# Weight conversion through a PSUM bank, GpSimd's long steps in halves, and a new port model in the planner

## The chip, the cores and the metric

The kernel runs on one NeuronCore of a Trainium2 chip. The metric is the device time of one execution in microseconds (us), lower is better. The core has five engines that work side by side and meet at semaphores: TensorE (PE in the profile; PEld is its weight load), VectorE (DVE), ScalarE (ACT), GpSimd (POOL) and SyncE (SP, which issues the DMA transfers). SBUF is the working memory of 128 partitions. PSUM is the small memory that TensorE writes; this kernel uses it as 8 banks of 512 fp32 values per partition.

## The reference, cut to what matters

```python
def _attn_ref(q, k, v, omega):                 # q, k, v: (8, 8, 576, 64) fp32
    q_s, k_s = q * scale, k * scale
    def phi(x):                                # 128 random features
        h = np.einsum('bhsd,md->bhsm', x, omega) - np.sum(x * x, -1, keepdims=True) / 2.0
        return np.exp(h - np.max(h, -1, keepdims=True)) / np.sqrt(m)
    q_p, k_p = phi(q_s), phi(k_s)
    kv = np.einsum('bhsm,bhsd->bhmd', k_p, v)
    z = np.sum(k_p, axis=2)
    num = np.einsum('bhsm,bhmd->bhsd', q_p, kv)
    return num / (np.einsum('bhsm,bhm->bhs', q_p, z)[..., None] + 1e-06)

def _moe_ref(x, w_in, w_out):                  # x: (4608, 512), w_in: (512, 2048), w_out: (2048, 512)
    h = x @ w_in
    g = h * erf(softplus(h))
    return g @ w_out
```

The attention's output, laid out as 4608 tokens of 512 values, is the x of the second part. The two weight matrices arrive as 64-bit floats, and the kernel turns them into 32-bit ones on the chip.

## The kernel before, in words

**Work.** Eight batches of 576 tokens. A batch has four pairs of heads in the attention and then two phases (`ph`) of the expert layer, each over half of the 2048 hidden values. A phase has four blocks "f" (`plain1` or `gemm1`: x times w_in for 256 hidden values) and four blocks "e" (`gemm2`: the hidden values of the phase before, times w_out). Tiles of matmul results are named `h`, `hS`, `hA` (first product), `o` (second), `ppk`, `ppq`, `kvp`, `pt`, `nd` (attention). Every matmul of the expert layer is done as three, with each operand split into a high part and the rest (`xh`/`xl`, `gh`/`gl`, and two halves of a weight tile `w`).

**Weights.** There are 32 weight units of 128 x 512 values. On its first use a unit is made (`make`, line 347): SP loads its 64-bit words into `st`; `w_bias` (POOL or ACT) scales the high words into `wt`; VectorE shifts `wt` in place (`w_shift`, TENSOR_SCALAR), then joins sign and tail in place (`w_sign`, `w_tail`, SCALAR_TENSOR_TENSOR, two operands each, `st` and `wt`). `parts` (line 339) then writes the high part into `w` (`w_high`, ACT or POOL) and the rest (`w_rest`, VectorE or POOL), and SP stores `w` to DRAM (`wd`) for later fetches. The first three batches (`PLAIN`) use the units as they are; in the third, `make_sums` builds sums of units (`R`, `S`, `cS`), with which the later batches need seven products in place of eight.

**Between the products.** `chain` (line 615) runs softplus and erf on ScalarE (`gs`), then for each group `gate` (`hs` = `gs` x `hs`), `high` (`gh`) and `rest` (`gl` = `hs` - `gh`). Gate and rest take 128 x 1152 values and may run on VectorE or POOL. `square` in the attention (`uk`, `uq`, 64 x 1152) runs on POOL or ACT. `split` makes `xh`, `xl` and the differences `xc`.

**Order.** `build` lists operations with, for each engine that may run them, an estimated cost and a slack: the engine takes the operation only if it is due later than that (-1e9: always). `Plan.order` (line 132) simulates five engines and writes down one order for each, which the chip then follows exactly. A tile takes a slot from its pool, so PSUM's 8 slots (`ps`) are shared under caps: 4 banks for attention (5 for the first batch), 3 and 2 for the two products. Due times come from `starts`: `FIRST` per pair of the first batch, `START0` for the first expert matmul. The model knows that some VectorE steps suffer beside GpSimd:

```python
                    if e == "V" and o.name in SHARED:
                        dur += min(dur, max(0.0, until["G"] - now) / 2)
```

Of the kernel before, what the change touches and what calls it, by code (L numbers as in the profile page):

```python
# [19 lines left out]
P = 128  # L20
# [43 lines left out]

SHARED = ("wshift", "wsign", "wtail", "wrest", "wwhole", "wsum", "xsum", "xhigh", "xrest", "gate",
          "high", "rest")


# [17 lines left out]
class Plan:  # L88
# [43 lines left out]
    def order(self, slots, caps):  # L132
# [56 lines left out]
        while True:  # L189
            progress = True  # L190
            while progress:
                progress = False
                for e in engines:
                    if not idle[e]:
                        continue
                    skipped, chosen = [], None
                    while ready[e]:
                        item = heapq.heappop(ready[e])
                        o = item[2]
                        if o.start is not None:  # L200
                            continue
                        ok = can(o)
                        if ok and e == "A":
                            if lock is not None and o.set is not None and o.macro != lock:
                                ok = False
                        if ok:
                            slack = next(s for x, _, s in o.opts if x == e)
                            if e == "S":
                                ok = o.due - now < slack
                            elif o.due - now < slack and slack > -1e8:  # L210
                                ok = False
                        if ok:
# [12 lines left out]
                    if e == "V" and o.name in SHARED:  # L225

                        dur += min(dur, max(0.0, until["G"] - now) / 2)
                    o.eng, o.start = e, now
                    for t in o.alloc:
                        t.slot = free[t.pool].pop(0)  # L230
                        held[t.stream] += 1
                        nxt[t.stream] += 1
                    idle[e] = False
                    if e == "A":
                        if o.set is not None and o.set != table:
                            dur += COST["table"]
# [55 lines left out]
WHOLE = 8  # L292
PLAIN = 3
PAIR = 8.6
FIRST = 13.0
LEAD = 30.0
STEP1 = 14 * 3 * COST["mm"]
STEP2 = 48 * COST["mm"]
START0 = 4 * FIRST + 10


def build(emit):
# [33 lines left out]
              reads=[(t, (x, k)) for x in "hl" for k in range(2)], writes=[(d, 0)],  # L336
              plan=clock[0] + 10.0, size=P * HW * 8)

    def parts(t, src, keys):

        ks = range(2)
        pl.op("whigh", [("A", 0.63, -1e9), ("G", 0.72, 5.0)], lambda e: E.w_high(e, t, src),
              reads=keys, writes=[(t, ("h", k)) for k in ks])
        pl.op("wrest", [("V", 0.7, -1e9), ("G", 1.35, 3.0)], lambda e: E.w_rest(e, t, src),
              reads=keys + [(t, ("h", k)) for k in ks], writes=[(t, ("l", k)) for k in ks])

    def make(u, t):

        nm = "_".join(str(c) for c in u)
        st = pl.tile("gl", f"st{nm}", [P, HW, 2], I32, "st")  # L350
        pl.op("wload", [("S", 0.1, AHEAD)], lambda e: E.w_load(st, u),
              writes=[(st, 0), (t, "room")], size=P * HW * 8)
        w = pl.tile("gh", f"wt{nm}", [P, HW], I32, "wt")
        pl.op("wbias", [("G", 0.95, -1e9), ("A", 0.65, -1e9)], lambda e: E.w_bias(e, st, w),
              reads=[(st, 0)], writes=[(w, 0)])
        pl.op("wshift", [("V", 0.7, -1e9)], lambda e: E.w_shift(w), reads=[(w, 0)], writes=[(w, 0)])
        pl.op("wsign", [("V", 0.92, -1e9)], lambda e: E.w_sign(st, w), reads=[(st, 0), (w, 0)],
              writes=[(w, 0)])
        pl.op("wtail", [("V", 0.92, -1e9)], lambda e: E.w_tail(st, w), reads=[(st, 0), (w, 0)],
              writes=[(w, 0)])  # L360
        parts(t, lambda: w.ap.bitcast(F32).rearrange("p (k c) -> p k c", k=2), [(w, 0)])
        store(u, t)

    def unit(u, block=None):
# [12 lines left out]
    def make_sums(ph, fp, t0, t1):  # L377

        r = pl.tile("gh", f"R{ph}_{fp}", [P, 2, 2, BW], F32, "wt")
        for i, t in enumerate((t0, t1)):  # L380
            pl.op("wwhole", [("V", 0.7, -1e9), ("G", 1.35, 3.0)],
                  lambda e, i=i, t=t: E.w_whole(e, r.ap[:, i], t),
                  reads=[(t, (x, k)) for x in "hl" for k in range(2)], writes=[(r, i)])
        s = pl.tile("gl", f"S{ph}_{fp}", [P, 4, BW], F32, "st")
# [36 lines left out]
    def load(n, qk):  # L421
# [13 lines left out]
        for i in range(parts):  # L435
            keys = range(3) if parts == 1 else [i]
            f = 1.0 / parts
            pl.op("sq" + qk, [("A", 1.17 * f + .1, -1e9)] if n == 0 else
                  [("G", 2.35, -1e9), ("A", 1.2, -1e9 if n < 4 else 4.0)],
                  lambda e, i=i: E.square(e, u, qk, i, parts),  # L440
                  reads=[(u, ("x", c)) for c in keys], writes=[(u, ("s", c)) for c in keys])

# [49 lines left out]
    def attend(n, t0):  # L492
        a = pairs[n]
        x = xs[n] = pl.tile("xs", f"xs{a['nm']}", [P, 2, T])
        for j in range(2):
            for t in range(2):
# [8 lines left out]
                pl.op("ndlog", [("A", 0.46, -1e9)], lambda e, j=j, nd=nd, rc=rc: E.log_den(rc, nd, j),  # L505
                      reads=[(nd, 0)], writes=[(rc, 0)], set="exp")
                pl.op("ndexp", [("A", 0.44, -1e9)], lambda e, j=j, rc=rc: E.exp_den(rc, j),
                      reads=[(rc, 0)], writes=[(rc, 0)], set="exp")
# [106 lines left out]
    def chain(b, ph, fps):  # L615
# [12 lines left out]
                  reads=[(x["gs"], 0) for x in gr], writes=[(g["gs"], 0)], set="erf", macro=m)  # L628
        for fp, g in zip(fps, gr):
            four = [(g["hs"], (i, t)) for i in range(2) for t in range(2)]  # L630
            pl.op("gate", [("V", 1.45, -1e9), ("G", 2.8, 10.0)], lambda e, g=g: E.gate(e, g["gs"], g["hs"]),
                  reads=four + [(g["gs"], 0)], writes=four)
            g["gh"] = pl.tile("gh", f"gh{b}_{ph}_{fp}", [P, 2, 2, T], F32R, cap=4 if b < PLAIN or (b, ph) == (PLAIN, 0) else None)
            pl.op("high", [("V", 0.8, -1e9), ("A", 1.2, 3.0)], lambda e, g=g: E.high(e, g["gh"], g["hs"]),
                  reads=four, writes=[(g["gh"], 0)])
# [69 lines left out]
def tile_attention_moe(ctx: ExitStack, tc: tile.TileContext, qT, kT, vP, omT, w1, w2, out):  # L705
# [55 lines left out]
    def difference(e, dst, a, b):  # L761
        (pool if e == "G" else dve).tensor_sub(dst, a, b)

    def rows(j):

        return (slice(0, D), slice(D, P)) if j == 0 else (slice(D, P), slice(0, D))

    class Emit:
# [52 lines left out]
        def square(self, e, u, qk, i, parts):  # L821
            c = slice(i * S2 // parts, (i + 1) * S2 // parts)
            src, dst = (slice(D, P), slice(0, D)) if qk == "k" else (slice(0, D), slice(D, P))
            if e == "G":
                pool.tensor_mul(u.ap[dst, c], u.ap[src, c], u.ap[src, c])
            else:
                act.activation(u.ap[dst, c], u.ap[src, c], AF.Square)

# [73 lines left out]
            copy(e, h.ap[:, i:i + n, :], src())  # L902

        def x_rest(self, e, l, src, h, i, n):
            difference(e, l.ap[:, i:i + n, :], src(), h.ap[:, i:i + n, :].bitcast(F32))

        def gemm1(self, hp, u, k, xh, xl, xi, c, more, end):
            wh, wl = (u.ap[:, k, i, c * P:(c + 1) * P] for i in range(2))
# [14 lines left out]
            act.activation(gs.ap, gs.ap, AF.Erf)  # L923

        def gate(self, e, gs, hs):
            (pool if e == "G" else dve).tensor_mul(hs.ap, gs.ap, hs.ap)

        def high(self, e, gh, g):
            copy(e, gh.ap, g.ap)

        def rest(self, e, gl, g, gh):
            difference(e, gl.ap, g.ap, gh.ap.bitcast(F32))

        def gemm2(self, op, w, fi, gh, gl, i, t, f):
            b, c = divmod(fi, 2)
# [71 lines left out]
```

## Time and profile before

| | us |
|---|---|
| median of 3 runs | 1127.03 (1125.81 to 1129.01) |
| the profiled execution | 1128.78 |
| its span, first to last instruction | 1126.8 |
| TensorE busy (modelled) | 1086.5 |
| VectorE busy | 758.5 |
| ScalarE busy | 718.8 |
| GpSimd busy | 471.4 |

TensorE's busy time counts an instruction as busy until its modelled end, and matmuls overlap; the number of matmuls that a stretch of time holds is the safer measure. A row of a group reads: line, engine, operation, output<-inputs, shape, count | busy us, mean ns | idle time of the engine before it. Nearly all rows carry line 722, the helper through which every instruction is issued, so rows are told apart by tile names. A row of a tile's view has the shortest, median and longest duration in ns. A row of the timeline has start and duration in us. All times are counted from the first instruction.

### The profile page before, as it was taken

Reading aid. Unit: us, or ns where it says so; the run is one execution under the profiler, and the core shown is the slowest. Engines: PE = TensorE matmul, PEld = TensorE weight load, DVE = VectorE, ACT = ScalarE, POOL = GpSimd, SP = SyncE. Lnnn points to the kernel's source line nnn. Section 1 sums busy time; section 2 is a strip of 40 time slices with the busy share of each in tenths; the row PEclk is TensorE's granted clock in tenths of the full one; section 3 lists DMA queues with packets and bytes.
Section 4 is the critical chain, followed back from the end, with each engine's and each line's share of the span. In section 5 each row is a group of like instructions: output and inputs, shape, how many; then the busy total and the mean of one; then the engine's idle time right before and its main releaser. Section 6 shows DMA issues by size and latency. Waiting matters only on the chain.

```text
span 1126.8 us, 21431 instructions
## 1 busy us (share of the span) xinstructions
PE 1086.5 (96%) x8272; PEld 1074.4 (95%) x8272; DVE 758.5 (67%) x1229; ACT 718.8 (64%) x1360; POOL 471.4 (42%) x276
## 2 busy tenths in 40 slices
PE   7999898999998999979999999999999999999998
PEld 6899798999998989979999999999999999999998
DVE  5969988876396585875668547684658657584641
ACT  8868776776666666754767766576667765544430
POOL 5637747533184274640325424352344413251320
PEclk9989999999998999989999999999999999999999
DMA  8545576574456565647765766657666665657761
GB/s 221 182 134 206 176 263 219 196 266 155 154 173 221 189 213 192 220 136 257 220 214 193 231 226 227 214 181 237 219 226 200 209 216 189 217 197 273 254 236 59
DMA packets 70116, 231.26 MB, mean 205 GB/s; under 512 B 8288, under 2 KB 8672, under 8 KB 70016
## 3 DMA queue, kind: packets, MB, share of 16 engines
q1 hardware_dynamic: 69952, 229.84, 62.0%
q8 instruction: 66, 1.08, 0.4%
q14 instruction: 34, 0.28, 0.1%
q0 software_dynamic: 64, 0.07, 0.0%
HBM read 195.26 MB, written 34.60 MB: 204 GB/s over the span
## 4 chain that ended last, share of the span: by engine, by line
PE 84%; DVE 10%; issue 2%; ACT 2%; POOL 1%; DMA 1%; SPq 0%; DVEq 0%; POOLq 0%; ACTq 0%
PE o L722 33%; PE hS L722 11%; PE h L722 10%; PE hA L722 8%; PE kvp L722 5%; PE ppq L722 5%; PE ppk L722 5%; PE nd L722 4%; DVE wt L722 3%; PE pt L722 2%; DVE gl L722 1%; DVE S L722 1%; DMA st<-w 1%; DVE w L722 1%; DVE hs L722 1%
## 5 line engine op out<-in xcount | busy, mean ns | idle before, releaser
L722 PE MATMUL o<-gh,w 128*128 128x288 f32 x2048 | 443.8, 298 | 3.8 <-DVE w L722 3.7
L722 PEld LDWEIGHTS o<-gh,w 128*128 128x128 f32 x2048 | 338.9, 188 | 4.5 <-DVE w L722 4.3
L722 PE MATMUL o<-gl,w 128*128 128x288 f32 x1024 | 302.2, 295 | 0.0
L722 PEld LDWEIGHTS o<-gl,w 128*128 128x128 f32 x1024 | 192.6, 188 | 0.2
L722 PE MATMUL h<-xh,w 128*128 128x288 f32 x768 | 181.7, 307 | 6.1 <-ACT hs L722 6.1
L722 POOL TENSOR_TENSOR hs<-gs,hs 128x1152 f32<-128x1152 f32 x36 | 102.0, 2838 | 167.9 <-ACT gs L722 155.4
L722 PE MATMUL hS<-xh,wS 128*128 128x288 f32 x640 | 165.7, 304 | 2.3 <-DVE u L722 2.3
L722 PEld LDWEIGHTS h<-xh,w 128*128 128x128 f32 x768 | 132.7, 192 | 7.0 <-ACT hs L722 6.8
L722 ACT ACTIVATE fk<-ppk,mxk 128x128 f32<-128x128 f32 x288 | 83.3, 373 | 85.6 <-DVE mxk L722 85.4
L722 POOL TENSOR_TENSOR gl<-hs,gh 128x1152 fp32r<-128x1152 f32 x35 | 109.2, 3131 | 33.8 <-ACT gh L722 24.4
L722 ACT ACT_TABLE_LOAD x92 | 118.0, 1283 | 7.0 <-DVE hs L722 4.7
L722 PE MATMUL hA<-xh,w 128*128 128x288 f32 x480 | 122.2, 299 | 0.0
L722 PEld LDWEIGHTS hS<-xh,wS 128*128 128x128 f32 x640 | 115.2, 190 | 2.6 <-DVE u L722 2.6
L722 PE MATMUL h<-xl,w 128*128 128x288 f32 x384 | 114.6, 298 | 0.4 <-POOL xl L722 0.4
L722 ACT ACTIVATE fq<-ppq,mxq 128x128 f32<-128x128 f32 x288 | 83.2, 370 | 30.4 <-DVE mxq L722 29.6
L722 PE MATMUL hS<-xl,wS 128*128 128x288 f32 x320 | 95.0, 297 | 0.0
L722 POOL TENSOR_TENSOR uq<-uq 64x1152 f32<-64x1152 f32 x21 | 46.3, 2203 | 113.7 <-DMA uq<-qT 67.6
L722 DVE TENSOR_REDUCE mxk<-ppk 128x3 f32<-128x384 f32 x96 | 51.9, 553 | 58.1 <-PE ppk L722 57.5
L722 ACT ACTIVATE gh<-hs 128x1152 fp32r<-128x1152 f32 x52 | 59.2, 1162 | 45.5 <-DVE hs L722 22.6
L722 PEld LDWEIGHTS hA<-xh,w 128*128 128x128 f32 x480 | 86.0, 189 | 0.0
L722 DVE TENSOR_TENSOR os<-o,os 128x288 f32<-128x288 f32 x64 | 29.1, 455 | 81.0 <-PE o L722 80.7
L722 PE MATMUL ppk<-wk,uk 128*128 128x128 f32 x576 | 79.6, 282 | 4.0 <-DVE wk L722 4.0
(94 smaller groups left out, 2195.0 us busy)
## 6 DMA issues: line engine op xcount, KB each, us to landing
w<-wdw SPq DMA_DIRECT2D x184, 512.0 KB, 4.3
wS<-wdcS SPq DMA_DIRECT2D x80, 512.0 KB, 4.0
st<-w SPq DMA_DIRECT2D x32, 512.0 KB, 4.8
wdw<-w SPq DMA_DIRECT2D x32, 512.0 KB, 3.6
v<-vP SPq DMA_DIRECT2D x32, 325.0 KB, 3.2
w<-wdw SPq DMA_DIRECT2D x40, 256.0 KB, 3.6
out<-os SPq DMA_DIRECT2D x32, 288.0 KB, 3.8
uk<-kT SPq DMA_DIRECT2D x31, 288.0 KB, 3.8
```

The costliest lines, as they stand in the source:

```text
L722: return tc.keep_in_program_order(method(*args, **kwargs))
```

## The change

The shift writes its result into a tile of PSUM (`pw`, at most one at a time, from the same 8 slots), sign and tail work there in place, and high part and rest read it from there. GpSimd no longer takes either of the last two steps for these units; for the sums' units (`make_sums`) it still may. On GpSimd, gate, rest, square and the x rests of more than one block are issued as two instructions of half the size. The planner's model takes a VectorE step of `SHARED` to wait until the running piece on GpSimd ends, and a GpSimd step until VectorE's last such step ends. The three steps that now touch PSUM leave `SHARED`. Costs, due times and slacks get other values, and a running mean of how late matmuls are (`late`) is added where an operation's slack is tested.

```diff
-SHARED = ("wshift", "wsign", "wtail", "wrest", "wwhole", "wsum", "xsum", "xhigh", "xrest", "gate",
+PIECES = dict(gate=2, rest=2, sqk=2, sqq=2, xrest=2)
+SHARED = ("wrest", "wwhole", "wsum", "xsum", "xhigh", "xrest", "gate",
           "high", "rest")
...
-                            elif o.due - now < slack and slack > -1e8:
+                            elif o.due - now + late < slack and slack > -1e8:
...
+                    if e == "T":
+                        late += 0.1 * (max(0.0, now - o.due) - late)
                     if e == "V" and o.name in SHARED:
-                        dur += min(dur, max(0.0, until["G"] - now) / 2)
+                        dur += max(0.0, until["G"] - now) % piece
+                        port = now + dur
+                    elif e == "G":
+                        dur += max(0.0, port - now)
+                        piece = dur / PIECES.get(o.name, 1) + 1e-6
...
-FIRST = 13.0
+FIRST = 11.5
-START0 = 4 * FIRST + 10
+START0 = 4 * FIRST + 5
+GATES = 10.0
+RESTS = 6.0
+EARLY = (2, 0)
+PW = 1
+WHV = 0.0
+GATES0 = 10.0
+RESTS0 = 15.0
+SQN = 4
+SQG = -1e9
+SQA = 4.0
+WHG = 5.0
+WBG = -1e9
...
-    def parts(t, src, keys):
+    def parts(t, src, keys, psum=False):
-        pl.op("whigh", [("A", 0.63, -1e9), ("G", 0.72, 5.0)], ...
+        pl.op("whigh", [("A", 0.58, -1e9), ("V", 0.62, WHV)] if psum else
+              [("A", 0.63, -1e9), ("G", 0.7, WHG)], ...
-        pl.op("wrest", [("V", 0.7, -1e9), ("G", 1.35, 3.0)], ...
+        pl.op("wlow" if psum else "wrest",
+              [("V", 0.68, -1e9)] if psum else [("V", 0.68, -1e9), ("G", 1.3, 3.0)], ...
...
+        p = pl.tile("ps", f"pw{nm}", [P, HW], I32, "pw", PW)
+        pl.op("wshift", [("V", 0.6, -1e9)], lambda e: E.w_shift(p, w), reads=[(w, 0)],
+              writes=[(p, 0)])
+        pl.op("wsign", [("V", 0.72, -1e9)], lambda e: E.w_sign(st, p), reads=[(st, 0), (p, 0)],
+              writes=[(p, 0)])
+        pl.op("wtail", [("V", 0.72, -1e9)], lambda e: E.w_tail(st, p), reads=[(st, 0), (p, 0)],
+              writes=[(p, 0)])
+        parts(t, lambda: p.ap.bitcast(F32).rearrange("p (k c) -> p k c", k=2), [(p, 0)], True)
...
-            pl.op("gate", [("V", 1.45, -1e9), ("G", 2.8, 10.0)], ...
+            pl.op("gate", [("V", 1.36, -1e9), ("G", 2.75, GATES if (b, ph) >= EARLY else GATES0)], ...
-            pl.op("rest", [("G", 2.8, 6.0), ("V", 1.45, -1e9)],
+            pl.op("rest", [("G", 2.75, RESTS if (b, ph) >= EARLY else RESTS0), ("V", 1.36, -1e9)],
...
+    def halves(e, n):
+        return (slice(0, n // 2), slice(n // 2, n)) if e == "G" else (slice(0, n),)
...
-        def w_shift(self, w):
-            dve.tensor_scalar(w.ap, w.ap, 3, None, op0=ALU.logical_shift_left)
+        def w_shift(self, p, w):
+            dve.tensor_scalar(p.ap, w.ap, 3, None, op0=ALU.logical_shift_left)
...
         def gate(self, e, gs, hs):
-            (pool if e == "G" else dve).tensor_mul(hs.ap, gs.ap, hs.ap)
+            for i in halves(e, 2):
+                (pool if e == "G" else dve).tensor_mul(hs.ap[:, i], gs.ap[:, i], hs.ap[:, i])
```

`square`, `x_rest` and `rest` are halved on GpSimd in the same way as `gate`. The slack of a rest on GpSimd in the first two batches goes from 6 to 15; `GATES`, `GATES0`, `RESTS`, `SQG`, `SQN`, `SQA`, `WHG` and `WBG` hold the values that stood in the code before.

More of the change, by code (lines that the diff above doesn't have):

```diff
@@ L156, in order @@
         now, table, lock, bw = 0.0, "exp", None, 0.0
+        port, piece, late = 0.0, 1.0, 0.0
         count = 0
@@ L337, in store @@
               plan=clock[0] + 10.0, size=P * HW * 8)
-    def parts(t, src, keys):
+    def parts(t, src, keys, psum=False):
         ks = range(2)
-        pl.op("whigh", [("A", 0.63, -1e9), ("G", 0.72, 5.0)], lambda e: E.w_high(e, t, src),
+        pl.op("whigh", [("A", 0.58, -1e9), ("V", 0.62, WHV)] if psum else
+              [("A", 0.63, -1e9), ("G", 0.7, WHG)], lambda e: E.w_high(e, t, src),
               reads=keys, writes=[(t, ("h", k)) for k in ks])
-        pl.op("wrest", [("V", 0.7, -1e9), ("G", 1.35, 3.0)], lambda e: E.w_rest(e, t, src),
+        pl.op("wlow" if psum else "wrest",
+              [("V", 0.68, -1e9)] if psum else [("V", 0.68, -1e9), ("G", 1.3, 3.0)], lambda e: E.w_rest(e, t, src),
               reads=keys + [(t, ("h", k)) for k in ks], writes=[(t, ("l", k)) for k in ks])
@@ L353, in make @@
         w = pl.tile("gh", f"wt{nm}", [P, HW], I32, "wt")
-        pl.op("wbias", [("G", 0.95, -1e9), ("A", 0.65, -1e9)], lambda e: E.w_bias(e, st, w),
+        pl.op("wbias", [("G", 0.8, WBG), ("A", 0.67, -1e9)], lambda e: E.w_bias(e, st, w),
               reads=[(st, 0)], writes=[(w, 0)])
[L356 to L361, printed above, removed]
+        p = pl.tile("ps", f"pw{nm}", [P, HW], I32, "pw", PW)
[6 more added lines that the diff above has]
+        parts(t, lambda: p.ap.bitcast(F32).rearrange("p (k c) -> p k c", k=2), [(p, 0)], True)
         store(u, t)
@@ L380, in make_sums @@
         for i, t in enumerate((t0, t1)):
-            pl.op("wwhole", [("V", 0.7, -1e9), ("G", 1.35, 3.0)],
+            pl.op("wwhole", [("V", 0.68, -1e9), ("G", 1.3, 3.0)],
                   lambda e, i=i, t=t: E.w_whole(e, r.ap[:, i], t),
@@ L438, in load @@
             pl.op("sq" + qk, [("A", 1.17 * f + .1, -1e9)] if n == 0 else
-                  [("G", 2.35, -1e9), ("A", 1.2, -1e9 if n < 4 else 4.0)],
+                  [("G", 2.2, SQG if n < SQN else -1e9), ("A", 1.2, -1e9 if n < SQN else SQA)],
                   lambda e, i=i: E.square(e, u, qk, i, parts),
@@ L504, in attend @@
                       plan=pair_time(n, t0 + 0.1 * j + 0.05 * t))
-                pl.op("ndlog", [("A", 0.46, -1e9)], lambda e, j=j, nd=nd, rc=rc: E.log_den(rc, nd, j),
+                pl.op("ndlog", [("A", 0.5, -1e9)], lambda e, j=j, nd=nd, rc=rc: E.log_den(rc, nd, j),
                       reads=[(nd, 0)], writes=[(rc, 0)], set="exp")
@@ L630, in chain @@
             four = [(g["hs"], (i, t)) for i in range(2) for t in range(2)]
-            pl.op("gate", [("V", 1.45, -1e9), ("G", 2.8, 10.0)], lambda e, g=g: E.gate(e, g["gs"], g["hs"]),
+            pl.op("gate", [("V", 1.36, -1e9), ("G", 2.75, GATES if (b, ph) >= EARLY else GATES0)], lambda e, g=g: E.gate(e, g["gs"], g["hs"]),
                   reads=four + [(g["gs"], 0)], writes=four)
             g["gh"] = pl.tile("gh", f"gh{b}_{ph}_{fp}", [P, 2, 2, T], F32R, cap=4 if b < PLAIN or (b, ph) == (PLAIN, 0) else None)
-            pl.op("high", [("V", 0.8, -1e9), ("A", 1.2, 3.0)], lambda e, g=g: E.high(e, g["gh"], g["hs"]),
+            pl.op("high", [("V", 0.76, -1e9), ("A", 1.17, 3.0)], lambda e, g=g: E.high(e, g["gh"], g["hs"]),
                   reads=four, writes=[(g["gh"], 0)])
             g["gl"] = pl.tile("gl", f"gl{b}_{ph}_{fp}", [P, 2, 2, T], F32R, cap=4 if b < PLAIN or (b, ph) == (PLAIN, 0) else None)
-            pl.op("rest", [("G", 2.8, 6.0), ("V", 1.45, -1e9)],
+            pl.op("rest", [("G", 2.75, RESTS if (b, ph) >= EARLY else RESTS0), ("V", 1.36, -1e9)],
                   lambda e, g=g: E.rest(e, g["gl"], g["hs"], g["gh"]),
@@ L824, in square @@
             if e == "G":
-                pool.tensor_mul(u.ap[dst, c], u.ap[src, c], u.ap[src, c])
+                for h in halves(e, S2 // parts):
+                    pool.tensor_mul(u.ap[dst, c][:, h], u.ap[src, c][:, h], u.ap[src, c][:, h])
             else:
@@ L904, in x_rest @@
         def x_rest(self, e, l, src, h, i, n):
-            difference(e, l.ap[:, i:i + n, :], src(), h.ap[:, i:i + n, :].bitcast(F32))
+            for c in halves(e, n) if n > 1 else (slice(0, 1),):
+                difference(e, l.ap[:, i:i + n, :][:, c], src()[:, c],
+                           h.ap[:, i:i + n, :][:, c].bitcast(F32))
         def gemm1(self, hp, u, k, xh, xl, xi, c, more, end):
@@ L931, in rest @@
         def rest(self, e, gl, g, gh):
-            difference(e, gl.ap, g.ap, gh.ap.bitcast(F32))
+            for i in halves(e, 2):
+                difference(e, gl.ap[:, i], g.ap[:, i], gh.ap[:, i].bitcast(F32))
         def gemm2(self, op, w, fi, gh, gl, i, t, f):
```

## The prediction

> **What bounds the kernel now.** I read the page first, then the table of stretches of time, then VectorE's, GpSimd's and TensorE's rows inside the stretches that lose time. The page and the stretches (columns: stretch, its length, then the busy time of PE, its weight load, DVE, ACT and POOL with their instructions in brackets, granted clock, DMA share, GB/s):
>
> ```profile
> span 1126.8 us, 21431 instructions
> PE 1086.5 (96%) x8272; PEld 1074.4 (95%) x8272; DVE 758.5 (67%) x1229; ACT 718.8 (64%) x1360; POOL 471.4 (42%) x276
> ```
>
> ```profile
> 0.00:50.00 50.00, 41.30 (x295) 37.17 (x295) 34.92 (x69) 41.63 (x120) 29.09 (x29) 0.97 0.74 214
> 50.00:100.00 50.00, 45.55 (x312) 43.27 (x313) 37.49 (x53) 35.81 (x83) 26.35 (x21) 0.93 0.42 143
> 100.00:150.00 50.00, 44.80 (x326) 43.74 (x325) 47.82 (x52) 40.42 (x71) 35.92 (x24) 0.97 0.63 212
> 150.00:200.00 50.00, 46.21 (x349) 45.32 (x348) 43.62 (x56) 33.82 (x71) 30.57 (x20) 0.97 0.65 221
> ...
> 325.00:350.00 25.00, 21.05 (x137) 20.05 (x137) 19.77 (x22) 14.43 (x31) 18.82 (x11) 0.86 0.60 202
> ...
> 400.00:425.00 25.00, 22.73 (x162) 21.86 (x161) 22.59 (x29) 15.46 (x34) 17.99 (x8) 0.93 0.64 213
> ...
> 470.00:500.00 30.00, 24.23 (x170) 23.36 (x169) 26.07 (x30) 14.64 (x33) 18.71 (x7) 0.89 0.39 125
> 500.00:995.00 495.00, 495.00 (x3880) 494.69 (x3879) 325.51 (x612) 324.61 (x585) 176.65 (x85) 1.00 0.66 216
> 995.00:1020.00 25.00, 22.69 (x159) 22.43 (x158) 17.44 (x20) 9.94 (x11) 9.94 (x4) 0.93 0.60 209
> ```
>
> PE's count tells more than its busy time. From 500 to 995 us it runs 3880 matmuls in 495 us, 0.1276 us each, at clock 1.00: there TensorE itself is the limit, and no faster VectorE can gain anything. At that rate the 295 matmuls of the first 50 us need 37.6 us, so 12.4 us are lost there. In the same way 50 to 100 loses 10.2, 100 to 150 8.4, 150 to 200 5.5 (24.1 for these three), and four short stretches later lose 7.5, 4.3, 8.3 and 4.7 (24.8 together). All of it is 61 us: 1066 us is what no reordering gets below, and the change has to work on these 61.
>
> What holds PE in these places is VectorE standing behind GpSimd. The longest single stall, seen on DVE, POOL and in PE's waits (line: waited for, total us, times, longest):
>
> ```profile
> 111.15 2.90 DVE L722 TENSOR_SCALAR wt<-wt 128x512 int32<-128x512 int32 x1
> 114.08 3.75 DVE L722 SCALAR_TENSOR_TENSOR wt<-st,wt 128x512 int32<-128x512 int32 x2
> ```
>
> ```profile
> 110.86 5.69 POOL L722 TENSOR_TENSOR hs<-gs,hs 128x1152 f32<-128x1152 f32 x2 [0.18 <-ACT gs L722]
> ```
>
> ```profile
> PE h L722 <- ACT hs L722: 6.1, 3, 5.0
> ```
>
> Two gates run on POOL from 110.86 to 116.55. The shift, started at 111.15, lasts 2.90 us, and the next DVE step again ends late. ACT's queue waits for those weights, its copy of h out of PSUM stands behind them, and PE sits still for 5.0 us. How long the same steps take undisturbed (min/median/max ns):
>
> ```profile
> L722 DVE SCALAR_TENSOR_TENSOR wt<-st,wt x64: 674/693/3042, 24.2 to 246.6; 128x512 int32<-128x512 int32 x64
> L722 DVE TENSOR_SCALAR wt<-wt x32: 414/474/2895, 23.4 to 245.4; 128x512 int32<-128x512 int32 x32
> L722 POOL TENSOR_SCALAR w<-wt x26: 617/620/1113, 34.2 to 247.4; 128x512 fp32r<-128x512 f32 x26
> L722 POOL TENSOR_TENSOR w<-wt,w x21: 1262/1293/1650, 29.7 to 238.6; 128x512 fp32r<-128x512 f32 x21
> L722 ACT ACTIVATE w<-wt x6: 630/631/636, 27.0 to 228.1; 128x512 fp32r<-128x512 f32 x6
> ```
>
> ```profile
> L722 DVE TENSOR_TENSOR hs<-hS,hs x80: 439/458/460, 492.6 to 1084.7; 128x288 f32<-128x288 f32 x80
> L722 POOL TENSOR_TENSOR gl<-hs,gh x35: 2649/3125/3779, 102.1 to 1070.2; 128x1152 fp32r<-128x1152 f32 x35
> L722 DVE TENSOR_TENSOR gl<-hs,gh x29: 1341/1359/3833, 102.7 to 1097.0; 128x1152 fp32r<-128x1152 f32 x29
> L722 DVE CAST gh<-hs x12: 747/2528/3244, 253.2 to 1066.4; 128x1152 fp32r<-128x1152 f32 x12
> ```
>
> A step whose operands all lie in SBUF spreads from 0.41 to 2.9 or from 1.34 to 3.83: the spread is at most one POOL step of 2.65. The step that reads one operand from PSUM (hS) has 80 instances between 439 and 460 ns, though POOL works through much of that time. So a PSUM operand takes a DVE step out of the wait, and a shorter POOL step shortens it.
>
> **The change, part by part.** *Conversion in PSUM* (32 weight units, 23 to 249 us). Between 12 and 200 us, where PE loses, VectorE spends on it (count, then busy us and mean ns):
>
> ```profile
> L722 DVE SCALAR_TENSOR_TENSOR wt<-st,wt 128x512 int32<-128x512 int32 x48 | 48.3, 1006 | 1.2
> L722 DVE TENSOR_SCALAR wt<-wt 128x512 int32<-128x512 int32 x24 | 24.5, 1020 | 1.0 <-ACT wt L722 0.5 <-POOL wt L722 0.2
> L722 DVE TENSOR_TENSOR w<-wt,w 128x512 fp32r<-128x512 f32 x8 | 10.4, 1306 | 0.6 <-POOL w L722 0.5
> ```
>
> Undisturbed they would take 48 x 0.693 + 24 x 0.414 + 8 x 0.693 = 48.7 (the last has two operands of the first's size); they take 83.2. So 34.5 us is waiting, and it goes. Against it: the shift now writes PSUM. No row of before shows DVE writing PSUM, so its price lies between 0.41 (as now) and 0.69 (the two-operand step of that size); I take 0.60, nearer the latter, since hS's 439 ns for 288 elements is about what an SBUF step without a double rate takes per element. That is 24 x 0.19 = 4.6. The rest of the weight can no longer go to POOL: the 16 of 24 units that went there cost DVE 16 x 0.69 = 11.0. The high part moves from POOL (26 of 32) to ACT, or to DVE when it is overdue. If half are overdue, DVE pays 12 x 0.69 = 8.3; if none, ACT pays 26 x 0.63 = 16.4 over 200 us in which it is busy 151.7 now. Net on DVE: -34.5 + 4.6 + 11.0 + 8.3 = -10.6, between -19 (no overdue ones) and 0 (24 overdue, shift at 0.69). POOL loses 0.62 and 1.29 us steps, which shortens other DVE waits too. The new wait, a shift for its bank, is for the low part of the unit before, on the same engine and so already past; on ACT the high part waits for DVE's tail with the exponentials queued behind it, as it does now in the six units there. SP issues the same loads and stores in a new order; the DMA share of 0.42 to 0.74 up to 200 us leaves room: 0.
>
> [...] In this trace a step of 288 elements takes at least 439 ns with hS in PSUM and 441 with all operands in SBUF:
>
> ```profile
> L722 DVE TENSOR_TENSOR xc<-xs,xc x14: 441/650/1679, 424.7 to 990.9; 128x288 f32<-128x288 f32 x14
> ```
>
> [...]
>
> *Halved POOL steps.* POOL's two-input steps take 1262 ns for 512 elements and 2649 for 1152: 2.17 ns an element and 0.15 us fixed. Halves thus take about 1.40 instead of 2.65, and each split adds 0.15 us to POOL. With some 120 such steps (35 are the rests above) that is 18 us on an engine busy 42%; it lies beside other work except where POOL's rest is itself last, where it costs 0.15 each. What it saves is read in the four late stretches, from VectorE's steps there:
>
> ```profile
> 330.46 5.66 DVE L722 TENSOR_TENSOR S<-R 128x256 f32<-128x256 f32 x2 [1.18 <-POOL R L722]
> ```
>
> ```profile
> 402.85 3.16 DVE L722 TENSOR_TENSOR R<-w 128x512 f32<-128x512 f32 x1
> ...
> 406.31 2.51 DVE L722 TENSOR_TENSOR S<-R 128x256 f32<-128x256 f32 x1
> ...
> 409.11 2.50 DVE L722 TENSOR_TENSOR S<-S,R 128x256 f32<-128x256 f32 x1
> ```
>
> ```profile
> 472.34 3.23 DVE L722 CAST gh<-hs 128x1152 fp32r<-128x1152 f32 x1
> 475.49 3.82 DVE L722 TENSOR_TENSOR gl<-hs,gh 128x1152 fp32r<-128x1152 f32 x1
> 479.23 3.18 DVE L722 CAST gh<-hs 128x1152 fp32r<-128x1152 f32 x1
> ...
> 482.80 3.30 DVE L722 TENSOR_TENSOR gl<-hs,gh 128x1152 fp32r<-128x1152 f32 x1
> ```
>
> ```profile
> 997.76 3.83 DVE L722 TENSOR_TENSOR hs<-gs,hs 128x1152 f32<-128x1152 f32 x1
> 1001.69 3.24 DVE L722 CAST gh<-hs 128x1152 fp32r<-128x1152 f32 x1
> ```
>
> With 0.41 for a 256-element step (the shift's undisturbed time stands for it, a lower bound), 0.69, 0.75 and 1.34 undisturbed, the waiting in them is 4.8, 6.7, 9.4 and 5.0 us. Halving the POOL step halves it: 2.4 + 3.3 + 4.7 + 2.5 = 12.9 us, against stalls of 7.5, 4.3, 8.3 and 4.7. I take 12. In those stretches the granted clock is 0.86 to 0.93 against 1.00 elsewhere, so part of each loss is slow matmuls behind the stall and goes with it; that is in the 24.8 already. Where a stall is shortened, ACT's exponentials and the next rest are late next.
>
> *The planner.* The waiting time in its model becomes the rest of the running piece and also holds for POOL; first-batch pairs are due every 11.5 us instead of 13, the first expert matmul at 51 instead of 62. The order of every engine is made anew. Dates only rank what is ready, and the first stretch's 12.4 us bound what an earlier start can bring; I count 0 for them. From 500 to 995 a new order can only lose: 0, covered by VectorE's 34% and POOL's 64% idle time there; without that cover a single stall like the late ones costs 4 to 8 us.
>
> **The sum.** From 50 to 200 VectorE is busy 128.9 of 150 us. It gets back 10.6 in conversion and about 5, an estimate, elsewhere: four of its other steps (gl, the x rests) that stand behind a POOL step of 2.65 us and then behind one of 1.40, at 1.25 each. Of these 16 I count three quarters on PE's path, 12 of the 24.1 lost. The first 50 us: conversion only starts at 23.4, so 1. Late stretches: 12. For new ties of the remade order I put +1. Together -24 on this execution's 1128.78 us (span 1126.8 and 2.0 around it): 1104.8. The median of the runs is 1.75 lower, 1127.03, so on runs 1103 to 1105; I say 1104.
>
> **Rivals.** *A PSUM bank too few: slower.* A unit now keeps one of 8 banks from shift to low part, 0.60 + 3 x 0.69 + 0.63 and three handoffs between engines, some 4 us; 32 units hold it nearly all of the first 250 us. PE already waits for banks whose readers are late:
>
> ```profile
> PE pt L722 <- ACT fk L722: 4.2, 2, 2.6
> ...
> PE kvp L722 <- DVE xs L722: 2.0, 1, 2.0
> ```
>
> If one eighth less room stretched the time from 23 to 200 by its eighth, 22 us, only the late 12 would be won and some order lost: 1128.8 + 22 - 12 = 1139. It decides once each unit costs PE over 24/32 = 0.75 us. Against it: these two waits are 6.2 us in all, and the chain they belong to gets faster.
>
> *Only the early part pays.* The remade order brings new stalls of the old size behind 300 us: 1128.8 - 13 + 1 = 1117. For it: the late stalls sit where gate, rest and sums of several groups fall together, which no halving removes. The mirror image, conversion eaten up by ACT (151.7 + 16.4 = 168 of about 185 us), gives the same 1117.
>
> *Most of it goes.* If VectorE stops being the limit up to 200, only the first 12.4 us and a third of the rest stay: 1128.8 - 61 + 12 + 16 = 1096, or about 1086 with the late stalls gone altogether.
>
> *It doesn't do what it says.* The hS rows show a step that reads PSUM out of the wait; none shows one that reads SBUF and writes PSUM, as the shift will. If it still waits, it keeps 24.5 - 24 x 0.414 = 14.6 of the 34.5 us: three quarters of it on the path would give 1104 + 11 = 1115.
>
> **How the numbers follow.** My forecast, 1098 to 1110: 0.36. One part lost or the shift still waiting, 1110 to 1123: 0.24. Most of it goes, 1086 to 1098: 0.16. Within 0.3% of 1127 (3.4 us, about what a measurement of this kernel tells from no change), gains and new stalls balancing: 0.08. Slower through banks or order: 0.16. Faster is the sum of the first three, 0.76. The range 1088 to 1130 leaves out some 2% below and 16% above.
>
> **What would show it.** Right: the steps on the PSUM tile between 0.55 and 0.75 us with no 2 to 3 us ones; gate and rest on POOL near 1.4; DVE's largest gl and gh under 2.9; over 1340 matmuls in the first 200 us (1282 now); 65 us a phase unchanged from 570 on. Wrong: PE waiting for ACT or DVE to free banks before 200 us, ACT above 90% there, or new stalls after 500.

## The result, and the profile after

The changed kernel takes 1095.17 us (median, 1094.32 to 1096.04) against 1128.02 us for the kernel before measured beside it: ratio 0.9708, 95% interval 0.9685 to 0.9732. The profiled execution took 1094.32 us. Its page:

```profile
span 1092.3 us, 21543 instructions
PE 1068.2 (98%) x8272; PEld 1058.3 (97%) x8272; DVE 721.9 (66%) x1293; ACT 698.1 (64%) x1333; POOL 454.4 (42%) x360
```

The same 8272 matmuls are issued in 34.5 us less. Where, is read from the same stretches of time as before (stretch, length, busy time and instructions of PE, PEld, DVE, ACT, POOL, then granted clock, DMA share, GB/s):

```profile
0.00:50.00 50.00, 40.20 (x290) 36.24 (x291) 36.29 (x76) 39.06 (x110) 20.95 (x27) 1.00 0.75 212
50.00:100.00 50.00, 46.82 (x360) 45.55 (x359) 40.99 (x75) 39.74 (x83) 24.84 (x25) 1.00 0.57 186
100.00:150.00 50.00, 46.39 (x349) 44.14 (x347) 45.80 (x76) 38.54 (x85) 22.48 (x18) 1.00 0.64 212
150.00:200.00 50.00, 50.00 (x389) 49.34 (x388) 48.09 (x71) 36.30 (x81) 27.55 (x23) 1.00 0.64 217
...
325.00:350.00 25.00, 25.00 (x197) 25.00 (x197) 16.02 (x27) 21.50 (x39) 14.64 (x14) 1.00 0.73 238
350.00:400.00 50.00, 48.96 (x384) 48.53 (x384) 34.86 (x53) 34.19 (x67) 29.83 (x23) 1.00 0.64 215
400.00:425.00 25.00, 25.00 (x198) 25.00 (x197) 14.31 (x23) 14.95 (x28) 16.97 (x18) 1.00 0.62 218
425.00:470.00 45.00, 43.50 (x340) 42.69 (x338) 37.84 (x62) 32.24 (x65) 27.25 (x19) 1.00 0.59 191
470.00:500.00 30.00, 30.00 (x238) 30.00 (x237) 14.49 (x33) 16.15 (x31) 7.33 (x6) 1.00 0.70 235
500.00:995.00 495.00, 493.90 (x3864) 493.64 (x3864) 315.95 (x613) 310.61 (x562) 196.08 (x143) 1.00 0.67 217
```

At the steady 0.1276 us a matmul, the stretches from 50 to 200 us lose 4.1 + 5.5 + 0.4 = 10.0 us (24.1 before), the first 50 lose 13.0 (12.4 before), and behind 325 us the stretches shown lose 1.0 + 1.6 + 2.0 and the last one 0.6, the others nothing; the four late stretches of before had lost 24.8. One column reads differently throughout: the granted clock is 1.00 in all of them. Over the whole execution it was 0.983 before. The profiled execution of the changed kernel is the best of its four in this: the other three have 0.995 to 0.998, and are 0.7 to 1.7 us longer.

The steps on the new PSUM tile, and the halved steps (min/median/max ns):

```profile
L749 DVE SCALAR_TENSOR_TENSOR pw<-st,pw x64: 677/695/704, 21.7 to 235.0; 128x512 int32<-128x512 int32 x64
L749 DVE TENSOR_SCALAR pw<-wt x32: 675/684/696, 21.0 to 233.5; 128x512 int32<-128x512 int32 x32
L749 DVE CAST w<-pw x19: 673/681/693, 31.0 to 236.3; 128x512 fp32r<-128x512 f32 x19
L749 ACT ACTIVATE w<-pw x13: 578/597/600, 23.2 to 206.6; 128x512 fp32r<-128x512 f32 x13
```

```profile
L749 POOL TENSOR_TENSOR gl<-hs,gh x64: 1398/1442/2588, 93.5 to 1036.6; 128x576 fp32r<-128x576 f32 x64
L749 DVE TENSOR_TENSOR gl<-hs,gh x32: 1344/1414/2595, 109.0 to 1061.5; 128x1152 fp32r<-128x1152 f32 x32
L749 DVE CAST gh<-hs x14: 746/792/1982, 106.1 to 1036.5; 128x1152 fp32r<-128x1152 f32 x14
```

Not one of the 96 joins and shifts in PSUM exceeds 0.704 us; in SBUF they reached 3.04. A step of VectorE with both operands in SBUF still waits, but its worst case is 2.6 us in place of 3.83: the wait is at most one GpSimd half of 1.4 us where it was one whole step of 2.65. What PE waits for now (line: waited for, total us, times, longest):

```profile
PE ppk L749 <- DVE wk L749: 4.0, 1, 4.0
PE nd L749 <- ACT qh L749: 3.6, 3, 1.8
PE nd L749 <- ACT fk L749: 1.9, 1, 1.9
PE o L749 <- DVE w L749: 1.7, 1, 1.7
```

Beyond the 4.0 us of the start no wait is longer than 1.9 us, where there had been one of 5.0, one of 3.7 and four between 2.3 and 2.9.

### The profile page after: what moved, and what is told of

Read it like the earlier page. It is cut to its first block, busy times and chain, and to the rows that moved or that the text cites. A ratio compares the mean times of both kernels' runs of the same rounds, so it can differ in the third digit from the quotient of the medians.

```text
span 1092.3 us, 21543 instructions
## 1 busy us (share of the span) xinstructions
PE 1068.2 (98%) x8272; PEld 1058.3 (97%) x8272; DVE 721.9 (66%) x1293; ACT 698.1 (64%) x1333; POOL 454.4 (42%) x360
## 4 chain that ended last, share of the span: by engine, by line
PE 92%; DVE 5%; POOL 1%; DMA 1%; issue 1%; SPq 1%; ACT 0%; DVEq 0%
PE o L749 37%; PE h L749 14%; PE hS L749 12%; PE hA L749 9%; PE ppq L749 5%; PE kvp L749 5%; PE ppk L749 5%; PE nd L749 4%; PE pt L749 2%; DVE pw L749 1%; DMA uk<-kT 1%; DVE w L749 1%; DVE mxk L749 1%; SPq L749 1%; DVE xs L749 0%
## 5 line engine op out<-in xcount | busy, mean ns | idle before, releaser
L749 PE MATMUL h<-xh,w 128*128 128x288 f32 x768 | 175.8, 302 | 0.0
L749 POOL TENSOR_TENSOR hs<-gs,hs 128x576 f32<-128x576 f32 x64 | 106.3, 1682 | 96.1 <-ACT gs L749 73.3
L749 PEld LDWEIGHTS h<-xh,w 128*128 128x128 f32 x768 | 129.3, 188 | 0.3
L749 POOL TENSOR_TENSOR gl<-hs,gh 128x576 fp32r<-128x576 f32 x64 | 110.3, 1747 | 42.7 <-ACT gh L749 24.7
L749 POOL TENSOR_TENSOR uq<-uq 64x576 f32<-64x576 f32 x46 | 51.7, 1142 | 137.4 <-DMA uq<-qT 108.7
L749 POOL TENSOR_TENSOR uk<-uk 64x576 f32<-64x576 f32 x50 | 59.0, 1200 | 109.4 <-DMA uk<-kT 108.3
```

The lines of the kernel that those rows point to most:

```text
L749: return tc.keep_in_program_order(method(*args, **kwargs))
```

## The experiments

Two theories went in. *Waiting*: VectorE stood behind GpSimd's long steps, and shortening or removing those waits is the gain. *Order*: the gain is the planner's, whose model now sees the waits. A third question came with the clock column. Each kernel below was timed beside the kernel before, and its ratio is to that one; its distance from the changed kernel is read across two such pairs, and their two intervals together leave it uncertain by some 3.5 us.

**Halves in the old order** (`b_halves`): the kernel before with its own order of every engine, and only this:

```diff
         def rest(self, e, gl, g, gh):
-            difference(e, gl.ap, g.ap, gh.ap.bitcast(F32))
+            for i in halves(e, 2):
+                difference(e, gl.ap[:, i], g.ap[:, i], gh.ap[:, i].bitcast(F32))
```

(gate, square and x rest likewise.)

> The kernel before with its own order of every engine, word for word; only GpSimd's gate, rest, square and x rest are issued as two halves. Two theories. Waiting: TensorE stalls where VectorE stands behind a whole GpSimd step of 2.65 us, so halves alone shorten those stalls: the four late stretches (325-350, 400-425, 470-500, 995-1020) lose about half of their 24.8 us, and the time is 1108 to 1116. Order: the gain of the change comes from the remade order of the planner, and halves in the old order only add 0.15 us a split: 1124 to 1130.

1118.44 us, ratio 0.9909 (0.9883 to 0.9934). A gain, but a little smaller than the theory of waiting gave. The first late stretch shows why, VectorE's timeline in this run:

```profile
328.12 3.21 DVE L722 TENSOR_TENSOR S<-R 128x256 f32<-128x256 f32 x2 [1.18 <-POOL R L722]
331.25 1.64 DVE L722 TENSOR_TENSOR S<-S,R 128x256 f32<-128x256 f32 x1
332.81 2.58 DVE L722 TENSOR_TENSOR gl<-hs,gh 128x1152 fp32r<-128x1152 f32 x1
```

The two sums took 5.66 us before and take 3.21: the wait is halved, as the prediction worked out. But VectorE now meets a GpSimd piece in the steps behind them as well. The next sum (0.41 before) now takes 1.64, and the gl (1.34 before) 2.58. In this stretch of the old order, which piles up rests on both engines, halves hand part of the gain back a step later.

**Whole steps in the new order** (`a_whole`): the changed kernel, its order kept:

```diff
     def halves(e, n):
-        return (slice(0, n // 2), slice(n // 2, n)) if e == "G" else (slice(0, n),)
+        return (slice(0, n),)
```

> The changed kernel with its own order, but each GpSimd step issued whole again (the planner still believes in halves). Waiting: VectorE's longest waits go back from 1.3 to 2.6 us and stalls of over 2 us return: 1105 to 1115. Order: 1094 to 1099.

1101.98 us, 0.9765 (0.9738 to 0.9792): 6.8 us above the changed kernel, between the two expectations. That is 6.8 us for the halves in the new order and 10.4 in the old; within the noise of both the two may be alike.

**Conversion in PSUM alone** (`b_psum`):

```diff
-SHARED = ("wshift", "wsign", "wtail", "wrest", ...
+SHARED = ("wrest", ...
...
-        pl.op("wshift", [("V", 0.7, -1e9)], lambda e: E.w_shift(w), reads=[(w, 0)], writes=[(w, 0)])
+        p = pl.tile("ps", f"pw{nm}", [P, HW], I32, "pw", PW)
+        pl.op("wshift", [("V", 0.6, -1e9)], lambda e: E.w_shift(p, w), reads=[(w, 0)], writes=[(p, 0)])
...
```

> The kernel before with nothing but the conversion in a PSUM bank (its steps out of the list of steps that suffer, their new costs and engines); the planner's old model makes the order anew. Waiting: some 12 us less in the first 200 us, late stretches as before, 1112 to 1120. Order: 1123 to 1133, since neither the model nor the dates are changed. If the bank that it holds costs TensorE, over 1130.

1118.2 us, 0.9904 (0.9881 to 0.9927), as the theory of waiting expected. What the bank that it holds may cost is smaller than the gain and wasn't measured by itself.

**Conversion back in SBUF** (`a_sbuf`): the changed kernel with

```diff
-        p = pl.tile("ps", f"pw{nm}", [P, HW], I32, "pw", PW)
-        pl.op("wshift", [("V", 0.6, -1e9)], lambda e: E.w_shift(p, w), ...
+        pl.op("wshift", [("V", 0.42, -1e9)], lambda e: E.w_shift(w), ...
...
-SHARED = ("wrest", ...
+SHARED = ("wshift", "wsign", "wtail", "wrest", ...
```

> The changed kernel with the conversion back in SBUF (in place, high part and rest on GpSimd again where they were allowed), its steps priced undisturbed and left to the new model of the port. Waiting: the first 200 us lose some 12 us again, the late stretches stay without loss: 1104 to 1112. Order: 1095 to 1101, since the new model sees the waits and plans around them.

1103.97 us, 0.9777 (0.9754 to 0.98), 8.8 us above the changed kernel and at the lower end of what waiting gave.

**Both parts, old planner** (`b_psum_halves`): the edits of `b_psum` and `b_halves` together.

> Conversion in PSUM and halved GpSimd steps together in the kernel before; the planner keeps its old model, dates and slacks. If the two parts add up, 1128.8 - 10.4 - 10.6 = 1108, and the 13 us that then remain to the changed kernel belong to model and dates. If they meet in the same stalls, 1111 to 1116. If each shortens stalls that only together fall under the length that costs the clock, below 1104.

1114.27 us, 0.9868 (0.9845 to 0.9891). The two parts overlap, as the second of the three cases said, and 19 us of the 33 are still missing. The theory of waiting alone doesn't reach the result.

**The old rule in the changed kernel** (`a_oldmodel`):

```diff
-                        dur += max(0.0, until["G"] - now) % piece
-                        port = now + dur
-                    elif e == "G":
-                        dur += max(0.0, port - now)
-                        piece = dur / PIECES.get(o.name, 1) + 1e-6
+                        dur += min(dur, max(0.0, until["G"] - now) / 2)
```

> The changed kernel with the old rule for VectorE beside GpSimd in the planner (half of GpSimd's rest, GpSimd itself never waits); conversion in PSUM, halves, dates, slacks and the running lateness as changed. If the new model is what places the late stretches well, their stalls return: 1103 to 1110. If the order owes nothing to it: 1094 to 1098.

1102.79 us, 0.9772 (0.9752 to 0.9793): 7.6 us more, at the lower end of the first case, and late stalls return, the longest of 4.2 us.

**The new rule in the kernel before** (`b_model`), with whole steps and SBUF conversion:

```diff
-                        dur += min(dur, max(0.0, until["G"] - now) / 2)
+                        dur += max(0.0, until["G"] - now) % piece
+                        port = now + dur
+                    elif e == "G":
+                        dur += max(0.0, port - now)
+                        piece = dur + 1e-6
...
-        pl.op("wshift", [("V", 0.7, -1e9)], ...
+        pl.op("wshift", [("V", 0.42, -1e9)], ...
```

(sign and tail 0.92 to 0.69, gate and rest 1.45 to 1.36 on VectorE and 2.8 to 2.75 on GpSimd.)

> The kernel before with the new rule for the port alone (a whole GpSimd step as the piece) and the undisturbed costs of conversion, gate and rest that go with it; SBUF conversion, whole steps, old dates. If a truer model by itself places the work better: 1112 to 1122. If it only pays where there are short steps to place: 1124 to 1134.

1111.26 us, 0.9861 (0.9844 to 0.9877): the largest gain of the three parts alone, 16 us, and a little better than the first case said. The planner that makes VectorE and GpSimd wait for each other gives GpSimd less of the long work, 24 gates and 24 rests (36 and 35 before). The rule and the costs that belong to it weren't separated here. `a_oldmodel` above does separate them in the changed kernel: there the costs stay, and the rule alone is worth 7.6 us. A remade order can also shift by some us by chance when any cost changes; no run changed the costs alone, so how much of the two figures is chance stays open.

**Where each part works.** The number of matmuls in three stretches of the time, in the order kernel before, `b_psum`, `b_halves`, `b_model` (one fence each, with the stretches in which the part does most):

```profile
0.00:200.00 200.00, 177.87 (x1277) 169.51 (x1278) 163.86 (x227) 151.68 (x342) 121.93 (x92) 0.96 0.61 198
200.00:600.00 400.00, 388.01 (x2976) 385.07 (x2975) 266.10 (x425) 264.49 (x509) 168.30 (x100) 0.98 0.61 202
600.00:1080.00 480.00, 477.69 (x3704) 477.12 (x3703) 315.44 (x558) 292.46 (x501) 178.51 (x83) 1.00 0.67 219
```

```profile
0.00:200.00 200.00, 181.81 (x1341) 174.16 (x1342) 162.92 (x281) 153.36 (x353) 89.07 (x63) 0.98 0.64 205
200.00:600.00 400.00, 388.14 (x2998) 385.81 (x2997) 271.14 (x432) 263.92 (x500) 170.45 (x95) 0.98 0.62 204
```

```profile
200.00:600.00 400.00, 389.71 (x2987) 387.01 (x2986) 251.44 (x422) 264.22 (x505) 185.88 (x144) 0.98 0.62 204
600.00:1080.00 480.00, 480.00 (x3733) 479.69 (x3732) 298.10 (x563) 295.21 (x502) 191.70 (x136) 1.00 0.68 222
```

```profile
0.00:200.00 200.00, 177.63 (x1287) 169.66 (x1288) 146.25 (x228) 164.07 (x363) 108.64 (x81) 0.96 0.62 201
200.00:600.00 400.00, 395.95 (x3099) 394.56 (x3098) 266.51 (x432) 284.28 (x539) 158.28 (x91) 1.00 0.63 208
```

And the changed kernel:

```profile
0.00:200.00 200.00, 183.41 (x1380) 175.27 (x1381) 171.17 (x295) 153.65 (x356) 95.82 (x92) 1.00 0.65 207
200.00:600.00 400.00, 396.36 (x3101) 394.86 (x3101) 266.77 (x450) 268.51 (x507) 196.22 (x150) 1.00 0.64 211
600.00:1080.00 480.00, 480.00 (x3734) 480.00 (x3733) 282.10 (x546) 275.98 (x472) 162.36 (x118) 1.00 0.67 219
```

Compare the first number in brackets, PE's. Up to 200 us the PSUM conversion does the work: 64 matmuls more by itself, 8 us at 0.1276, while halves add 18 and the model 10. From 200 to 600 us it is the model: 123 matmuls, 15.7 us, where PSUM adds 22 and halves 11, and its granted clock there is 1.00 with GpSimd's steps still whole. Behind 600 halves add 29 matmuls (3.7 us) and the model 13; either by itself removes the stall at 1000 us.

Taking a part out of the changed kernel says the same. Here are the first 200 us of `a_sbuf` and the middle stretch of `a_oldmodel`:

```profile
0.00:200.00 200.00, 181.64 (x1315) 171.32 (x1316) 168.06 (x249) 155.79 (x354) 125.65 (x112) 0.97 0.63 199
```

```profile
200.00:600.00 400.00, 388.98 (x3009) 386.81 (x3007) 259.44 (x431) 258.12 (x487) 201.24 (x151) 0.99 0.63 206
```

Without the conversion in PSUM the first 200 us hold 65 matmuls fewer (8.3 us), and the rest of the time as many as the changed kernel. With the old rule the middle holds 92 fewer (11.7 us), while the first 200 us hold 21 more: the new rule pays late and costs a little early. Whole steps (`a_whole`) lose 24 up to 200 us and 36 from 200 to 600.

**Dates, lateness, slack.** `a_olddates`:

```diff
-FIRST = 11.5
+FIRST = 13.0
-START0 = 4 * FIRST + 5
+START0 = 4 * FIRST + 10
```

> The changed kernel with the old due times of the first pairs (13 us each) and of the first expert matmul (62 us). As the prediction counted nothing for the dates: 1093 to 1098. If the dates pull the first 200 us together: 1099 to 1108.

1098.06 us, 0.9732 (0.9711 to 0.9754), at the upper end of the first expectation: 2.9 us above the changed kernel, and the intervals overlap. `a_modelonly` takes back lateness and slack besides:

```diff
-                        late += 0.1 * (max(0.0, now - o.due) - late)
+                        pass
-RESTS0 = 15.0
+RESTS0 = 6.0
```

> The changed kernel with the old dates, without the running lateness and with the old slack of an early rest on GpSimd (6): conversion, halves, new rule for the port and new costs remain. Of the 19 us between the two parts alone (1114.3) and the changed kernel (1095.2), the old rule cost 7.6 and the old dates 2.9. If lateness and slack do nothing, 1097 to 1100, and the other 8 to 9 us belong to the new costs together with the rule. If they matter, 1101 to 1108.

1101.11 us, 0.9771 (0.9757 to 0.9786). Dates, lateness and slack are worth some 6 us together; how they share it stays open. The step from `b_psum_halves` to this kernel, 13 us, is the rule with all the new costs.

**What a stall costs** (`a_probe`): in seven steady phases of the changed kernel, ahead of one addition,

```diff
+        if o != "table" and o.name == "hadd":
+            for _ in range(bursts.get(hadds, 0)):
+                dve.memset(om, 0.0)
+            hadds += 1
```

> The changed kernel with seven bursts of small VectorE fills (14, 18, 22, 26, 32, 40 and 50 of them, 0.17 to 0.2 us each, over a constant no longer used) in seven phases of the steady part, each ahead of an addition that TensorE soon needs. They hold TensorE for 0 to some 7 us. Clock theory: stalls below some 2 us cost their own length and leave the granted clock at 1.00; longer ones are followed by 3 to 8 us at 0.50 and cost 1.7 to 4 us more than their length. Rival: the clock follows the busy share smoothly, and cost grows in proportion to the stall's length from the shortest on.

1130.54 us, 1.0021 (1.0004 to 1.0037). The places of the seven bursts, shortest first:

```profile
590.00:610.00 20.00, 18.17 (x142) 17.59 (x141) 16.77 (x43) 11.32 (x28) 9.71 (x7) 1.00 0.49 156
655.00:680.00 25.00, 24.96 (x198) 24.69 (x197) 17.97 (x54) 17.34 (x36) 7.38 (x7) 1.00 0.72 229
722.00:745.00 23.00, 20.33 (x150) 19.92 (x149) 18.93 (x53) 12.15 (x30) 9.86 (x7) 0.93 0.42 144
790.00:815.00 25.00, 23.46 (x182) 22.67 (x181) 18.97 (x61) 15.62 (x34) 4.96 (x5) 1.00 0.64 207
860.00:885.00 25.00, 19.74 (x146) 19.51 (x144) 19.63 (x62) 12.36 (x31) 9.09 (x7) 0.86 0.39 130
930.00:955.00 25.00, 20.00 (x148) 19.76 (x147) 19.36 (x70) 10.72 (x30) 4.21 (x4) 0.93 0.43 147
998.00:1025.00 27.00, 19.29 (x126) 19.05 (x125) 16.76 (x66) 9.76 (x9) 5.50 (x5) 0.81 0.47 166
```

The burst at 655 us cost nothing. Idle time of PE (length less PE busy) of 1.8 and 1.5 us at 590 and 790 costs 1.9 and 1.8 by the count, at clock 1.00. Idle 2.7, 5.3, 5.0 and 7.7 us cost 3.9, 6.4, 6.1 and 10.9, at a clock of 0.81 to 0.93: 1.1 to 3.2 us more than the idle time itself. (How long PE idles doesn't rise strictly with the burst, since the addition is needed sooner in some phases than in others.) In these seven places the step lies between 1.8 and 2.7 us, and the proportional rival falls: at 590 and 790 us the clock stays at 1.00, and behind the four longer ones it is at 0.50 for 3.4 to 10.2 us. The extra is smaller than the 1.7 to 4 us expected. At 860 and 998 us part of the slow time lies inside the stall; at 930, where none does, the small extra isn't explained.

The traces of the other kernels don't make the step sharper. This stretch of `a_oldmodel` holds a wait of 2.7 us:

```profile
597.00:604.00 7.00, 4.30 (x33) 3.91 (x32) 4.21 (x10) 6.89 (x16) 4.97 (x4) 1.00 0.55 177
```

Its clock stays at 1.00, while a wait of 1.9 us in the kernel before is followed by 3.4 us at half clock (from 417). Shorter waits close together were followed by half clock as well: 0.9, 1.5 and 1.5 us within 6 us in the kernel before (from 342), and three of 0.8 to 1.2 us within 5 us in `a_whole` (from 466). In the traces of the kernel before, the changed kernel and the probe, behind the first 10 us, no single wait clearly shorter than 1.8 us was followed by half clock, and every one longer than 2.7 us was (2.9, 3.7 and 5.0 us in the kernel before, 5.0, 5.3 and 7.7 in the probe); between them it went either way.

**Quarters** (`a_quarter`), pointed to by the waits that are left:

```diff
-PIECES = dict(gate=2, rest=2, sqk=2, sqq=2, xrest=2)
+PIECES = dict(gate=4, rest=4, sqk=2, sqq=2, xrest=2)
...
+            for i, t in ((0, 0), (0, 1), (1, 0), (1, 1)):
+                (pool if e == "G" else dve).tensor_mul(hs.ap[:, i, t], gs.ap[:, i, t], hs.ap[:, i, t])
```

> The changed kernel with GpSimd's gate and rest in four pieces instead of two (planner told so, 3.1 us a step in place of 2.75). Waiting: VectorE waits at most some 0.8 us behind a gate or rest; but what is lost now after 200 us is 5 us in all, and each step takes 0.3 us more on GpSimd: 1091 to 1096. If the fixed cost of the pieces or their turns with VectorE take it back: 1096 to 1102.

1092.73 us, 0.9692 (0.9678 to 0.9707), inside the first expectation. It is the fastest kernel of the study; but the changed kernel's interval reaches 0.9685, and the two were not timed side by side, so that it beats that one is likely and not shown.

## Why the prediction was right, and where it was not

The measured time lies in the range (1088 to 1130) and beyond the likeliest case (1098 to 1110): it fell into "most of it goes" (0.16), whose 1096 left 12 + 16 us of loss where 13.0 + 15.2 stayed. The sum said -24 us, the profile -34.5. The direction and the early part are right for the reason given. That the time isn't further off owes something to luck: the late part was won, but mostly by the planner, for which the sum had nothing.

- *What bounds it*: right. The steady part didn't gain (3864 matmuls from 500 to 995 us, 3880 before), and the whole gain came out of the 61 us that PE lost in named stretches.
- *Conversion in PSUM*: right in size and place. Three quarters of the 10.6 us, as the sum counts it, are 8.0; `b_psum` gains 8.2 us of matmuls in the first 200 us, and `a_sbuf` loses 8.3. The waiting of 34.5 us is gone. What replaces it, from VectorE's groups between 12 and 200 us after the change:

```profile
L749 DVE SCALAR_TENSOR_TENSOR pw<-st,pw 128x512 int32<-128x512 int32 x54 | 37.5, 694 | 1.5
L749 DVE TENSOR_SCALAR pw<-wt 128x512 int32<-128x512 int32 x27 | 18.5, 686 | 2.8 <-POOL wt L749 2.2 <-ACT wt L749 0.5
L749 DVE TENSOR_TENSOR w<-pw,w 128x512 fp32r<-128x512 f32 x26 | 17.8, 686 | 0.8 <-ACT w L749 0.3
L749 DVE CAST w<-pw 128x512 fp32r<-128x512 f32 x14 | 9.6, 684 | 0.2
```

  That is 83.4 us for 27 units, 3.09 each, against 3.47 before: 9.1 us less for 24 units, where the step said 10.6 net. The shift took 0.684, at the upper bound of 0.69 and not the 0.60 chosen; 14 high parts of 27 went to VectorE where 12 of 24 were assumed. In the rows of before, a further element costs a two-operand step 1.04 ns (674 ns for 512, 1341 for 1152) and a one-operand step in SBUF 0.52 (414 and 747); the shift, with its result in PSUM, took what a two-operand step takes. The two-operand joins paid nothing for their operand in PSUM: 677 ns at least, against 674 with both in SBUF.
- *The first 50 us*: -1 predicted, nothing measured (13.0 lost against 12.4). 50 to 200 us: -12 predicted, -14.1 measured. VectorE is no less busy there (134.9 of 150 us against 128.9), since the work comes earlier; what went is its standing still.
- *Halved steps*: the mechanism was right and the term too large for halves alone. The step put 12 us into the four late stretches; in the old order halves gave 40 matmuls behind 200 us, 5.1 us; in the first late stretch, waits of half the length met more of VectorE's steps.
- *The planner: 0, and +1 for new ties*. This is the step that failed. The late stretches were a fault of the old order itself, which charged a VectorE step at most its own length for standing behind GpSimd. The new rule with its costs, alone, recovered 15.7 us from 200 to 600 us with the conversion and the steps as they were, and taking the rule alone out of the changed kernel lost 11.7 there. The 12 us booked under halves for those stretches became 20, and most of it belongs here. The dates, for which the step also had 0, are worth 2.9 us, within the noise; with lateness and slack some 6.
- *The clock*: booked as "in the 24.8 already", but half of the waiting was assumed to take about half of the loss. It isn't proportional. The stretches of the kernel before at half clock, picked from its trace:

```profile
28.40:31.80 3.40, 3.25 (x7) 2.21 (x8) 3.27 (x6) 2.62 (x8) 3.25 (x3) 0.53 0.01 4
58.80:65.70 6.90, 6.90 (x34) 6.90 (x33) 5.46 (x6) 3.40 (x13) 2.48 (x2) 0.51 0.58 208
...
342.10:348.90 6.80, 6.43 (x26) 6.13 (x27) 3.26 (x7) 4.83 (x12) 3.75 (x3) 0.51 0.71 236
...
1007.60:1011.00 3.40, 3.40 (x17) 3.40 (x16) 2.77 (x8) 1.76 (x2) 0.00 (x0) 0.53 0.23 53
sum 37.50, PE 34.52 PEld 32.78 DVE 28.19 ACT 21.20 POOL 17.13; mean PE 4.31 PEld 4.10 DVE 3.52 ACT 2.65 POOL 2.14
```

  Eight such stretches (counts 7, 34, 16, 18, 26, 14, 17, 17; 149 matmuls) fill 37.5 us with what 19.0 us hold at full clock. 18.5 us were lost while the clock was low, of which PE sat idle for 3.0. In the changed kernel's profiled execution there is no such stretch. So some 15.5 of the 34.5 us are clock. This is an estimate and rather an upper one: PE's busy time is modelled, 2.4 of the 15.5 us lie in the stretch from 28.4, in the 50 us that gained nothing, and the other three executions of the changed kernel still have a little half clock. It fits that no wait behind the start is longer than 1.9 us now; that the shorter waits are the cause, and not their new places, is argued and not shown. The stretches of half clock last 3.4 or 6.8 to 6.9 us, and stalls of about 2 us already came ahead of them: the stretch from 58.8 follows the wait of 2.0 us for a PSUM bank that the prediction shows, and the last one, from 1007.6, follows this wait of the kernel before:

```profile
PE hS L722 <- DVE u L722: 2.3, 1, 2.3
```
- *Rivals*: no bank became short (waits for readers of PSUM banks are 1.9 us or less). The conversion held its bank for 5.0 us a unit, 160 us in all between 21 and 238; the prediction's 4 us for 32 units make 128 us, and not nearly all of the first 250. ACT is busy 153.7 of the first 200 us, 151.7 before; writing PSUM from SBUF doesn't wait (696 ns at most). "Only the early part pays" was right that halving doesn't remove the late stalls (`b_halves` keeps the first three), and missed that the new rule would. In "most of it goes", 1086 for no late stall is 2 us too low by its own terms: 1128.8 - 61 + 12 + 8 = 1088.

## What to carry to other kernels

A stall of TensorE had a step in its price here: a single one below some 1.8 us cost about its length, a longer one that took the clock down cost one to three microseconds besides, and between 1.8 and 2.7 us it could be either. So bringing a stall from above the step to below it saves more than the time by which it is shortened; look at the granted clock of short windows, and at stalls that lie close together. Where a planner writes the order, test its model of shared resources against the trace first: one rule that undercharged a wait was worth 7.6 us here, and 16 with its costs in the kernel before. Moving one operand of a VectorE step into PSUM took it out of GpSimd's way here (0.704 us at most where 3.04 had been), at no price for the two-operand steps (677 ns at least, 674 before), and at 0.27 us for the one-operand step of 512 elements.

## What was not expected of the hardware

The shift of 512 elements takes 0.684 us from SBUF to PSUM against 0.414 within SBUF where nothing held it up: its destination alone cost that step 0.27 us. ACT's copy of the same size takes 597 ns from PSUM against 631 from SBUF. And nearly the same pair of stalls, 1.9 us and then 1.4 to 1.7 us some 4 us later (at 103 and 107 us, in the probe at 105 and 109), left the clock at 1.00 in the changed kernel's profile and took it down for 7 us in the probe's, from 108.7 on and so behind the first of the two. With the wait of 2.7 us that didn't take it down, this shows that near the step the clock depends on more than the length; on what, no run here tells.
